# One core, attention and gated unit: head sums on ScalarE, seeded value blocks, joined tails, and a new written order

## The chip, the core and the metric

The kernel runs on one core of a Trainium2 chip. Its time is the device time of one execution in microseconds (us); a kernel's figure is the median of its runs. TensorE multiplies, and writes its results into eight accumulator banks; VectorE and ScalarE read those banks and work element by element; GpSimd and SyncE (SP) mostly issue transfers, and GpSimd also takes powers and copies a few rows. Every engine runs its own list of instructions in order and waits where an operand is not there yet.

## What is computed

Eight batches, eight heads, 576 tokens, head width 64, so 512 channels:

```python
kv  = einsum('bhsd,bhse->bhde', k, v)          # 64x64 per head
out = einsum('bhsd,bhde->bhse', q, kv)
x   = out / sqrt(mean(out*out, -1) + 1e-6) * g_norm    # per head
x   = x.transpose(0, 2, 1, 3).reshape(8, 576, 512)
gate = sigmoid(causal 5-tap convolution of x along the tokens, per channel)
return (gate * (x @ w_val)) @ w_out
```

q, k, v and g_norm are float32. The three weights are double precision and are narrowed to float32 on the chip.

## The kernel before

All work is a list of named steps, PLAN, in an order that is written out: a loop runs it from front to back, each step appends its instructions to the engines' lists, and numbers behind an @ say which of a few fixed buffers (rooms) a new tile takes. So the order of the steps is the order on every engine and every queue. `bank` tiles are the eight accumulator banks.

Per batch b:

- `load_half` brings k or v in two halves of head pairs, `load_q` or `load_q_rows` brings q. `kv_product` makes k'v (L476), `kv_copy` (or `kv_half` for batch 0) moves it out of the bank. `turn_q` (VectorE, L500) or `turn_q_rows` with `sort_q` (TensorE L515 and copies L534, batches 0 and 1) turn q so that the head width lies on the partitions.
- `raw_pair` (two chunks of 128 tokens), `raw_tail` (the last 64 tokens) and, for batch 0, `raw_half` multiply q by kv (L551, L563). A batch has four chunks c = 0 to 3 and the tail c = 4.
- `square` (ScalarE, L600) squares a chunk into a buffer that has one more column per head, holding 64 times 1e-6; `sums` (VectorE, L607) adds up each head's 65 columns; `powers` (GpSimd, L617) raises the sums to −0.5; `normalise` scales: for batch 0 one VectorE instruction per chunk (L626), for the others one ScalarE instruction per chunk and head with the root as a per-partition scale (L636).
- The result is turned so that channels lie on partitions: `turn_x` (TensorE, L648) with `keep_x` (L655) for batches 0 and 1 and for tails, `turn_blocks` (VectorE, L661) with `move_blocks` (transfers, half on SP, half on GpSimd, L669) otherwise. `halo` copies the convolution's earlier rows (GpSimd).
- `gate_start` (ScalarE, L680), four `gate_tap` (VectorE, L686) and `gate_end` (sigmoid on ScalarE, L693) for each of four channel blocks.
- Value product: batches 0 and 1 by `val_product` (L698), each output block the sum of four products with the four row blocks of w_val. From batch 2 on `val_fast` (L747) makes four output blocks from seven products of sums instead of eight: bank a takes products 0, 2, 4 and 6 one on top of the other and is read out between them, b takes product 3, c takes 1 and 5. `x_sums`, `val_sums` make the sums (VectorE); `val_keep` n copies (ScalarE, n = 0, 1, 2, 6) or adds (VectorE, n = 3, 4, 5, L754) into gv.
- `gated` multiplies gate and value (L711). Output: `fast_product i p n` (L838), again seven products, for batches 2i and 2i+1, with `token_sums`, `weight_sums` and `fast_keep`. The 64-token tails of two batches are done together by `out_product i 8` (L785), a plain product with 64 columns of weights per batch, and `keep_out`. `store` writes the rows.
- The weights: `stage_weight` loads one of four column blocks; `narrow_weight ... n` turns it in steps n = 0 to 7, of which 1, 2 and 3 are three ScalarE passes over the exponents (L405, L407, L409) and the others VectorE passes. `start_warm` only multiplies the identity, to occupy TensorE.

The order around the change is given by PLAN alone. Transfers are issued by SP in PLAN's order, except that q's second half and v of batch 0 go by ScalarE's queue, and half of `move_blocks`, the convolution weights and g_norm by GpSimd's.

Of the kernel before, what the change touches and what calls it, by code (L numbers as in the profile page):

```python
# [9 lines left out]
FP32 = mybir.dt.float32  # L10
# [9 lines left out]
load_q_rows 0 1; load_q_rows 0 0; load_half v 0 0 @ 0; load_half k 0 0 @ 0; load_half v 0 1 @ 0;  # L20
load_half k 0 1 @ 0; start_warm 5 256 @ 0; warm_up; stage_weight wval 0; stage_weight wval 1;
stage_weight cw 0 @ 0; turn_q_rows 0 4 @ 1; turn_q_rows 0 3 @ 2; sort_q 0 4 @ 0; turn_q_rows 0 0 @ 3;
turn_q_rows 0 2 @ 4; sort_q 0 3; turn_q_rows 0 1 @ 5; start_warm 3 256 @ 6; load_q_rows 1 0; load_q_rows 1 1;
sort_q 0 0; stage_weight wval 2; kv_product 0 0 @ 7 0; narrow_weight cw 0 0 @ 0; load_half k 1 1; sort_q 0 2;
load_half v 1 1; kv_half 0 0; sort_q 0 1; raw_half 0 3 0 @ 1; narrow_weight cw 0 1; narrow_weight cw 0 2;
kv_product 0 1; stage_weight wval 3; narrow_weight cw 0 3; load_half k 1 0; narrow_weight cw 0 4;
narrow_weight cw 0 5 @ 0; raw_half 0 0 0 @ 2; stage_weight wout 1 @ 1; narrow_weight cw 0 6 @ 1; kv_half 0 1;
narrow_weight cw 0 7; narrow_weight wval 0 0 @ 1; raw_half 0 3 1; narrow_weight wval 0 5 @ 2;
narrow_weight wval 0 1; raw_half 0 0 1; narrow_weight wval 0 6 @ 3; turn_cw @ 6; square 0 3 @ 0;
raw_half 0 2 0 @ 3; keep_cw; square 0 0 @ 1; sums 0 3 @ 0 0; raw_half 0 2 1; narrow_weight wval 0 2;  # L30
raw_half 0 4 1 @ 4; sums 0 0; powers 0 3; load_half v 1 0; square 0 2 @ 2; raw_half 0 4 0;
narrow_weight wval 1 0 @ 0; raw_half 0 1 0 @ 5; square 0 4 @ 0; sums 0 2; narrow_weight wval 0 3;
raw_half 0 1 1; sums 0 4; load_half v 2 1 @ 0; start_warm 1 256 @ 0; narrow_weight wval 1 1;
narrow_weight wval 0 4; powers 0 2; square 0 1 @ 1; narrow_weight wval 1 5 @ 0; narrow_weight wval 1 2;
narrow_weight wval 0 7; stage_weight wout 0 @ 2; turn_q_rows 1 3 @ 7; normalise 0 3 @ 0;
narrow_weight wval 1 3; turn_q_rows 1 2 @ 6; sums 0 1; sort_q 1 3 @ 1; turn_q_rows 1 1 @ 0;
load_half v 2 0 @ 0; narrow_weight wval 2 0 @ 1; turn_x 0 3 @ 1; narrow_weight wval 1 6 @ 1; powers 0 1;
normalise 0 4 @ 1; narrow_weight wval 2 1; turn_q_rows 1 0 @ 7; load_q 2 2; normalise 0 2 @ 2; turn_x 0 4 @ 4;
keep_x 0 3; narrow_weight wval 1 4; turn_x 0 2 @ 3; keep_x 0 4; narrow_weight wval 2 2;
narrow_weight wval 2 5 @ 2; kv_product 1 1 @ 1 4; narrow_weight wval 1 7; keep_x 0 2;  # L40
narrow_weight wval 2 6 @ 3; sort_q 1 1; val_product 0 1 1 @ 3; narrow_weight wval 3 0 @ 0;
narrow_weight wval 3 5 @ 0; halo 0; normalise 0 1 @ 0; narrow_weight wval 3 1; normalise 0 0 @ 1;
narrow_weight wval 2 3; narrow_weight wval 3 6 @ 1; turn_x 0 1 @ 0; narrow_weight wval 3 2; turn_x 0 0 @ 5;
narrow_weight wval 2 4; load_half k 2 1 @ 0; val_product 0 0 1 @ 2; keep_x 0 1; narrow_weight wout 1 5 @ 2;
# [186 lines left out]
def kernel(  # L231
# [22 lines left out]
    HALO = (K - 1) * TB  # L254
    SX = HALO + S
    HB = P // TB
    NV = 2
    NR = S // D
    SV = S // NV
    ACT_NORM = range(1, B)  # L260
    WHOLE = (0,)
    TURNED_X = 2
    FAST_VAL = 2
    FAST_OUT = 0
    PAIRED_Q = (0, 1)
    ACT_SUMS = ()
# [69 lines left out]
    def head(hp, r):  # L336

        return r * (H // 2) + hp
# [579 lines left out]
```

## Time and profile before

| | |
|---|---|
| three runs | 295.33 us median (295.32 to 295.54) |
| profiled execution, first to last instruction | 294.9 us |
| TensorE busy | 287.0 us, 97% |
| VectorE busy | 268.7 us, 91% |
| ScalarE busy | 198.7 us, 67% |
| GpSimd busy | 120.7 us, 41% |
| first value product (L698) starts | 26.97 us |
| last product ends | 290.5 us |
| four tail products (L785) | 14.6 us |
| 32 head sums of eight heads (L607) | 21.6 us |

The profile takes one execution. Busy time counts an engine from the start of an instruction to its end, overlaps once. A group's line gives source line, engine, operation, what is written from what, shapes, count, busy time, mean ns of one, and the engine's idle time before it with what ended it. The chain follows back from the last instruction what released each step. A float32 product is recorded as two matmul records, a transpose as one.

### The profile page before, as it was taken

The page shows a single profiled execution, that of the slowest core. Times are in us where ns is not written, and L with a number is a line of the kernel's source. Part 1 is how long each engine was busy: PE and PEld are TensorE (multiplying, and loading weights), DVE is VectorE, ACT ScalarE, POOL GpSimd, SP SyncE. Part 2 cuts the span into 40 slices and gives each one's busy share as a digit, 9 for nine tenths or more (in the row PEclk, how much of TensorE's full clock was granted, in tenths as well). Part 3 has the DMA queues.
Part 4 walks back from the last instruction along what each step waited for, and adds up shares of the span by engine and source line. Part 5 has one row for each costly group of instructions (what it writes and reads, how often), then busy time and mean ns, then how long its engine had stood idle before and what let it go on. Part 6 is the DMA issues. An engine that isn't in the chain of part 4 may idle for free.

```text
span 294.9 us, 8675 instructions
## 1 busy us (share of the span) xinstructions
PE 287.0 (97%) x3279; PEld 226.9 (77%) x3279; DVE 268.7 (91%) x483; ACT 198.7 (67%) x621; POOL 120.7 (41%) x131
## 2 busy tenths in 40 slices
PE   7999999999999999999999999999999999999994
PEld 3776878788887768878887767888887588788583
DVE  1699999999999999999999999999998999999812
ACT  2899999999786667867477576659588433723330
POOL 3067054854491477421881649021592072000020
PEclk9997999999999999999999999999999999999999
DMA  7999998886686766946789789534553170221344
GB/s 268 379 392 410 284 276 230 239 258 176 197 189 198 234 150 182 341 144 174 182 237 279 167 218 308 165 112 109 141 128 80 44 170 2 57 53 36 98 105 120
DMA packets 32009, 55.51 MB, mean 188 GB/s; under 512 B 6166, under 2 KB 14358, under 8 KB 31968
## 3 DMA queue, kind: packets, MB, share of 16 engines
q1 hardware_dynamic: 29328, 49.50, 57.2%
q0 software_dynamic: 1760, 3.43, 5.2%
q10 hardware_dynamic: 880, 2.03, 1.8%
q8 instruction: 26, 0.43, 0.6%
q14 instruction: 15, 0.12, 0.1%
HBM read 39.21 MB, written 9.44 MB: 165 GB/s over the span
## 4 chain that ended last, share of the span: by engine, by line
PE 94%; DMA 2%; ACT 1%; DVE 1%; issue 0%
PE bank L838 33%; PE bank L747 28%; PE bank L698 11%; PE bank L476 7%; PE bank L551 6%; PE bank L785 5%; PE bank L648 2%; DMA qs<-in_q_dram 2%; PE bank L563 2%; PE bank L515 1%; PE bank L464 0%; ACT wexp L409 0%; DVE x L626 0%; ACT sq L596 0%; DVE ss L607 0%; ACT wexp L407 0%
## 5 line engine op out<-in xcount | busy, mean ns | idle before, releaser
L617 POOL TENSOR_TENSOR rt<-ss,mhalf 128x8 f32<-128x8 f32 (+3 forms) x38 | 73.1, 1937 | 82.0 <-DVE ss L607 81.8
L686 DVE SCALAR_TENSOR_TENSOR gate<-xT,cwT,gate 128x576 f32<-128x576 f32 x128 | 100.4, 807 | 0.2
L636 ACT ACTIVATE x<-bank,rt 128x64 f32<-128x64 f32 x252 | 56.1, 375 | 3.5 <-POOL rt L617 3.2
L838 PE MATMUL bank<-wsum,w 128*128 128x256 f32 x192 | 47.3, 381 | 0.0
L669 POOL DMA_DIRECT2D xT<-y x48 | 26.6, 559 | 41.6 <-DVE gv L754 13.5
L838 PEld LDWEIGHTS bank<-wsum,w 128*128 128x128 f32 x192 | 36.0, 190 | 6.1 <-issue 0.8
L747 PE MATMUL bank<-xs,vsum 128*128 128x288 f32 x144 | 37.1, 407 | 0.0
L747 PEld LDWEIGHTS bank<-xs,vsum 128*128 128x128 f32 x144 | 27.3, 190 | 7.3
L698 PE MATMUL bank<-xT,wval 128*128 128x288 f32 x128 | 32.8, 411 | 0.0
L838 PE MATMUL bank<-wout,gv 128*128 128x256 f32 x128 | 32.3, 382 | 0.0
L698 PEld LDWEIGHTS bank<-xT,wval 128*128 128x128 f32 x128 | 24.0, 192 | 6.3
L693 ACT ACTIVATE gate<-gate 128x576 f32<-128x576 f32 x32 | 23.0, 727 | 7.9 <-DVE gate L686 7.8
L838 PEld LDWEIGHTS bank<-wout,gv 128*128 128x128 f32 x128 | 24.0, 190 | 3.5
L680 ACT ACTIVATE gate<-xT,cwT 128x576 f32<-128x576 f32 x32 | 25.2, 804 | 0.9 <-DVE gv L711 0.9
L747 PE MATMUL bank<-xT,wval 128*128 128x288 f32 x96 | 25.7, 406 | 0.0
L600 ACT ACTIVATE sq<-bank 128x256 f32<-128x256 f32 (+1 forms) x70 | 21.6, 400 | 6.0 <-PE bank L551 5.8
L711 DVE TENSOR_TENSOR gv<-gv,gate 128x576 f32<-128x576 f32 x32 | 23.5, 745 | 2.0 <-ACT gate L693 1.5
L607 DVE TENSOR_REDUCE ss<-sq 128x8 f32<-128x520 f32 (+1 forms) x40 | 24.7, 624 | 0.5 <-ACT sq L600 0.4
L848 DVE TENSOR_TENSOR ot<-bank,ot 128x256 f32<-128x256 f32 (+1 forms) x32 | 17.2, 546 | 8.4 <-PE bank L838 4.1
L747 PEld LDWEIGHTS bank<-xT,wval 128*128 128x128 f32 x96 | 18.2, 190 | 4.5
L854 ACT COPY ot<-bank 128x256 f32<-128x256 f32 x16 | 6.0, 376 | 22.6 <-PE bank L838 22.6
L551 PEld LDWEIGHTS bank<-kv,qT 64*64 64x64 f32 x1008 | 16.3, 135 | 4.8 <-issue 2.1
(91 smaller groups left out, 469.4 us busy)
## 6 DMA issues: line engine op xcount, KB each, us to landing
qs<-in_q_dram SPq DMA_DIRECT2D x96, 140.0 KB, 4.0
out_dram<-ot SPq DMA_DIRECT2D x136, 64.0 KB, 1.7
k<-in_k_dram SPq DMA_DIRECT2D x14, 576.0 KB, 4.9
v<-in_v_dram SPq DMA_DIRECT2D x12, 576.0 KB, 5.3
xT<-y POOLq DMA_DIRECT2D x48, 64.0 KB, 2.7
xT<-y SPq DMA_DIRECT2D x48, 64.0 KB, 2.7
y<-in_moe_w_val_dram SPq DMA_DIRECT2D x4, 512.0 KB, 11.9
w<-in_moe_w_out_dram SPq DMA_DIRECT2D x4, 512.0 KB, 7.1
```

What stands on the lines that cost most here:

```text
L551: nc.tensor.matmul(st["raw", b, c][r][cols, to * D:(to + 1) * D], st["qT", b][rows, hp, first:first + D], kvs[b % 2][rows, hp, :], start=T ...
L607: nc.vector.reduce_sum(out=st["ss", b][:, FIRST[c]:FIRST[c] + n], in_=st["sq", b, c][:, 0:n], axis=AX.X)
L617: nc.gpsimd.tensor_tensor(out=st["rt", b][:, which], in0=st["ss", b][:, which], in1=mhalf[:, which], op=ALU.pow)
L636: nc.scalar.activation(out=x[:, to * D:(to + 1) * D], in_=raw[:, h * D:(h + 1) * D], func=AF.Copy, scale=root[:, to:to + 1])
L669: (nc.sync if i % 2 else nc.gpsimd).dma_start(out=xTs[b % 2][i * TB:(i + 1) * TB, :, first:first + P], in_=y[a * TB:(a + 1) * TB, i])
L680: nc.scalar.activation(out=gate[:], in_=xTs[b % 2][:, jt, HALO:SX], func=AF.Copy, scale=cwT[:, K - 1, jt:jt + 1])
L686: nc.vector.scalar_tensor_tensor(out=gate[:], in0=xTs[b % 2][:, jt, tap * TB:tap * TB + S], scalar=cwT[:, tap, jt:jt + 1], in1=gate[:], op ...
L693: nc.scalar.activation(out=gate[:], in_=gate[:], func=AF.Sigmoid)
L698: nc.tensor.matmul(val[:], wval[:, kc, jt * P:(jt + 1) * P], xTs[b % 2][:, kc, HALO + n * SV:HALO + (n + 1) * SV], start=(kc == 0), stop=( ...
L711: nc.vector.tensor_tensor(out=both, in0=both, in1=st["gate", b, jt][:], op=ALU.mult)
L747: nc.tensor.matmul(st[bank, "val", b, mj][:], weights_[:, k], tokens()[:, k], start=(n in (0, 1, 3) and k == 0), stop=(k == NK // 2 - 1), ...
L838: nc.tensor.matmul(st[bank, i, p], tokens()[:, k], weights_[:, k], start=(n < 2 and k == 0), stop=(k == NK // 2 - 1), skip_group_check=True)
```

## The change

- *Head sums.* For batches 1 to 7 `square` makes one ScalarE instruction per head, whose accumulator output is the head's sum; the squares themselves go to a scrap buffer. `sums` is gone for them, and GpSimd adds 64 times 1e-6 before the power.
- *Batch 0 in whole-array units.* Four units (two chunk pairs by two halves of the heads) of two chunks each: `raw_unit`, `square_unit`, `sums_unit`, `powers_unit`, `normalise_unit`, `turn_unit`, `keep_unit`. A unit needs only half of the heads' kv. `val_product` of batch 0 can run in two halves; the weights' row blocks are paired as 0, 2 and 1, 3 (EARLY, LATE) in place of 0, 1 and 2, 3.
- *Loads.* The second half of k of batch 0 is loaded behind the first column block of w_val; later loads change places as well.
- *Seeded value blocks.* In twelve blocks `val_keep 0` copies bank a into bank b, and product 3 is accumulated on top; then one copy replaces the addition.
- *Joined tails.* `keep_tail` gathers the tails of two batches; two such pairs go through the seven-product form as `fast_product 4 0 n` and `5 0 n`; `out_product` and `keep_out` are no longer in the list.
- *Narrowing.* Steps 2 and 3 become one VectorE pass (minimum, then times 2^23).
- *Choice of engine.* Many copies, `normalise` and `gate_start` take a flag that puts them on VectorE; `move_blocks` is split into its SP and GpSimd halves.
- The whole PLAN is written in a new order.

```diff
-load_q_rows 0 1; load_q_rows 0 0; load_half v 0 0 @ 0; load_half k 0 0 @ 0; load_half v 0 1 @ 0;
-load_half k 0 1 @ 0; start_warm 5 256 @ 0; warm_up; stage_weight wval 0; stage_weight wval 1;
...
+load_q_rows 0 0; load_q_rows 0 1; start_warm 1 248 @ 0; load_half k 0 0 @ 0; load_half v 0 0 @ 0; load_half v 0 1 @ 0;
...
+kv_product 0 0 @ 2 3; kv_half 0 0 0; start_warm 1 254 @ 4; stage_weight wval 0; load_half k 0 1 @ 0; turn_cw @ 1;
+kv_half 0 0 1 1; raw_unit 0 0 @ 5; keep_cw; narrow_weight wval 0 5 @ 2; sort_q 0 1; narrow_weight wval 0 0 @ 1;
...
+powers 5 1; normalise 5 1 @ 2; store 0 7; gate_tap 3 2 3; fast_product 1 0 2; turn_blocks 5 0; fast_keep 1 0 2;
...
+fast_keep 3 3 4; store_last 3 6 0; start_warm 1 244 @ 7; fast_product 3 3 6; store_last 3 6 1; fast_keep 3 3 6 1;
+store_last 3 7 1; store_last 3 7 0
...
-    ACT_SUMS = ()
-    ROOTS = {(0, 2): H + H // 2, (0, 1): 2 * H}
+    ACT_SUMS = (1, 2, 3, 4, 5, 6, 7)
+    SEEDED_OUT = set()
+    SEEDED_VAL = {(4, 0), (7, 1), (2, 1), (3, 1), (6, 1), (7, 0), (2, 0), (5, 1), (3, 0), (5, 0), (6, 0), (4, 1)}
...
+    def copy(e, out, in_):
+
+        if e:
+            nc.vector.tensor_copy(out=out, in_=in_)
+        else:
+            nc.scalar.copy(out=out, in_=in_)
...
         elif n == 2:
-            nc.scalar.activation(out=e, in_=e, func=AF.Relu, bias=biases[0:rows, 1:2], scale=-1.0)
-        elif n == 3:
-            nc.scalar.activation(
-                out=e, in_=e, func=AF.Identity, bias=biases[0:rows, 2:3], scale=-float(1 << 23))
+            nc.vector.tensor_scalar(
+                out=e, in0=e, scalar1=MOST, scalar2=float(1 << 23), op0=ALU.min, op1=ALU.mult)
...
         if b in ACT_SUMS:
             new_sums(b)
+            first = columns(b, c).start
             for r, raw in enumerate(st["raw", b, c]):
                 for h in range(n // 2):
                     to = r * n // 2 + h
                     nc.scalar.activation(
-                        out=sq[:, to, 0:D], in_=raw[:, h * D:(h + 1) * D], func=AF.Square,
-                        accum_out=st["ss", b][:, FIRST[c] + to:FIRST[c] + to + 1])
+                        out=junk[:, h], in_=raw[:, h * D:(h + 1) * D], func=AF.Square,
+                        accum_out=st["ss", b][:, first + to:first + to + 1])
             return
...
+    def root(b, which):
+        ss, rt = st["ss", b][:, which], st["rt", b][:, which]
+        if b in ACT_SUMS:
+            nc.gpsimd.tensor_scalar_add(ss, ss, D * EPS)
+        nc.gpsimd.tensor_tensor(out=rt, in0=ss, in1=mhalf[:, which], op=ALU.pow)
...
+    def raw_unit(g, i):
+
+        raw = st["unit", g, i] = ps([P, 2, C // 2], f"unit{g}_{i}")
+        for j, c in enumerate(UNIT[g]):
+            for m in range(2):
+                nc.tensor.matmul(
+                    raw[:, j, m * P:(m + 1) * P], st["qT", 0][:, 2 * i + m, c * P:(c + 1) * P],
+                    kv_bd[:, 2 * i + m, :], start=True, stop=True)
...
+    def normalise_unit(g, i):
+        x = st["ux", g, i] = new("x", [P, 2, C // 2], FP32, f"ux{g}_{i}")
+        roots = st["rt", 0][:, unit_columns(g, i)]
+        for j in range(2):
+            scaled(x[:, j].rearrange("p (r h e) -> p r h e", r=2, e=D), st["unit", g, i][:, j],
+                   roots[:, j * H // 2:(j + 1) * H // 2])
+
+    def turn_unit(g, i):
+        px = st["upx", g, i] = ps([P, 2, 2, P], f"upx{g}_{i}")
+        for j in range(2):
+            for r in range(2):
+                nc.tensor.transpose(px[:, r, j, :], st["ux", g, i][:, j, r * P:(r + 1) * P], ident[:])
...
-    def val_product(b, jt, n):
-        val = ps([P, SV], f"val{b}_{jt}_{n}")
-        for kc in range(NK):
+    def val_product(b, jt, n, i=None):
+        if ("val", b, jt, n) not in st:
+            st["val", b, jt, n] = ps([P, SV], f"val{b}_{jt}_{n}")
+        for kc in range(NK) if i is None else (i, i + NK // 2):
...
+        begins = (0, 1) if (b, mj) in SEEDED_VAL else (0, 1, 3)
+        if n in begins:
             st[bank, "val", b, mj] = ps([P, SV], f"v{bank}{b}_{mj}")
...
+    def val_keep(b, mj, n, on=0):
+        seeded = (b, mj) in SEEDED_VAL
+        if seeded and n == 0:
+            st["b", "val", b, mj] = ps([P, SV], f"seed{b}_{mj}")
...
         if n == 0:
-            nc.scalar.copy(out=to(0, 0), in_=a)
+            copy(on, out=b_ if seeded else to(0, 0), in_=a)
...
+        elif n == 3 and seeded:
+            copy(on, out=to(0, 0), in_=b_)
...
+    def keep_tail(b, on=0):
+
+        if ("tail", b // 2) not in st:
+            st["tail", b // 2] = new("sq", [P, NK, P], FP32, f"tail{b // 2}")
+        first = b % GVS * S + SF
+        copy(
+            on, out=st["tail", b // 2][:, :, b % 2 * T:(b % 2 + 1) * T], in_=gv[:, :, first:first + T])
...
+        chunk = lambda r, k: lambda: (
+            gv[:, k, begin + r * P:begin + (r + 1) * P] if i < B // 2 else st["tail", 2 * (i - B // 2) + r][:, k])
```

More of the change, by code (lines that the diff above doesn't have):

```diff
@@ L576, with columns @@
     FIRST = {3: 0, 2: H, 4: 2 * H, 1: 2 * H + H // 2, 0: 3 * H + H // 2}
+    def columns(b, c):
+        first = NJ * H if b in WHOLE else FIRST[c]
+        return slice(first, first + heads(c))
     def new_sums(b):
@@ L654, in keep_x @@
         px = st["px", b, c][:].rearrange("p k t -> p (k t)")[:, 0:NK * m]
[L655 to L658 removed]
+        copy(on, out=xTs[b % 2][:, :, first:first + m], in_=px.rearrange("p (k t) -> p k t", k=NK))
     def turn_blocks(b, c):
@@ L859, in fast_keep @@
         else:
-            last = (i, p) == (B // 2 - 1, 2 * NV - 1)
-            (nc.vector.tensor_copy if last else nc.scalar.copy)(out=second[:, LOW], in_=a)
+            copy(on, out=second[:, LOW], in_=a)
     def store_last(i, c, n):
```

644 lines of the change are left out of this document (333 added, 311 removed).

## The prediction

> **What bounds the kernel now.** I read the page first, then the busy time by stretches, the groups of instructions, the chain in order of time, and for prices the timeline of ScalarE.
>
> ```profile
> span 294.9 us, 8675 instructions
> PE 287.0 (97%) x3279; PEld 226.9 (77%) x3279; DVE 268.7 (91%) x483; ACT 198.7 (67%) x621; POOL 120.7 (41%) x131
> PE 94%; DMA 2%; ACT 1%; DVE 1%; issue 0%
> ```
> ```profile
> core 0: us, PE busy (x) PEld busy (x) DVE busy (x) ACT busy (x) POOL busy (x), PEclk, DMA share, GB/s
> 0.00:27.00 27.00, 23.49 (x320) 16.57 (x320) 17.43 (x57) 20.05 (x50) 11.70 (x14) 0.95 0.97 357
> 27.00:80.00 53.00, 53.00 (x897) 42.87 (x894) 52.08 (x92) 50.05 (x159) 23.46 (x20) 0.99 0.85 247
> 80.00:140.00 60.00, 60.00 (x741) 48.24 (x740) 59.93 (x105) 44.33 (x151) 30.76 (x33) 1.00 0.71 201
> 140.00:220.00 80.00, 80.00 (x1005) 64.83 (x1004) 79.42 (x136) 52.85 (x180) 42.08 (x46) 1.00 0.69 187
> ```
> ```profile
> L607 DVE TENSOR_REDUCE ss<-sq 128x8 f32<-128x520 f32 x32 | 21.6, 679 | 0.1
> L636 ACT ACTIVATE x<-bank,rt 128x64 f32<-128x64 f32 x252 | 56.1, 375 | 3.5 <-POOL rt L617 3.2 <-DVE y L661 0.3
> ```
> ```profile
> 17.89 0.39 ACT sq L596
> 18.28 0.61 ACT wexp L409
> 18.89 0.61 ACT wexp L405
> 21.40 0.68 DVE ss L607
> 104.55 3.58 PE bank L785 x16
> 206.62 12.29 PE bank L838 x56
> 290.56 0.42 DVE ot L861
> ```
> ```profile
> DVE wexp L400 <- DMA w<-in_moe_conv_w_dram: 6.8, 1, 6.8
> ```
> ```profile
> 46.92 1.74 ACT L636 ACTIVATE x<-bank,rt 128x64 f32<-128x64 f32 x8
> 49.71 1.12 ACT L655 ACTIVATE xT<-bank 128x512 f32<-128x512 f32 x2
> 146.35 1.21 ACT L600 ACTIVATE sq<-bank 128x256 f32<-128x256 f32 x4 [0.27 <-PE bank L551]
> ```
>
> TensorE is busy for all of 27 to 290.6 us and holds 94% of the chain: its list of work sets the end. VectorE is full beside it until 220 us, ScalarE almost full until 80. Only the head (3.5 us of TensorE idle, plus warm-up products) and the last 4.3 us are anything else; from 17.9 to 24 us the chain runs over ScalarE and VectorE.
>
> A row's mean includes overlap with the next instruction, so I price by distances from start to start: a 64-column activation 0.20 us ((1.74 − 0.375)/7), a head-sum reduce 0.60, a gate tap 0.73. With such prices I counted both written orders. "Behind" is an engine's work listed before a step; "lost" is the step's start minus it.
>
> Before, at raw_tail 1, 2, 3, 4, 7 (starts 37.7, 75.5, 103.0, 133.4, 232.1 us): TensorE has 22.8, 60.0, 87.0, 117.4, 215.7 us behind it, so it has lost 14.9, 15.5, 16.0, 16.0, 16.4; VectorE 26.0, 64.2, 91.6, 121.9, 219.0, lost 11.7, 11.3, 11.4, 11.5, 13.1; ScalarE at the first two 30.3 and 66.8, lost 7.4 and 8.7. At the last product TensorE has done 273.7 and lost 16.8.
>
> **The change, part by part.**
>
> *Joined tails.* Four tail products (4 × 3.58 = 14.3 us of TensorE) become two seven-product blocks, 56 records; the chain row of exactly 56 such records is 12.3 us, and 56 × 0.216 is 12.1. On the path: −2.1. VectorE gets eight half-size sums (2.7) and the blocks' additions (1.9); ScalarE eight tail copies (2.2) and loses four 0.48 copies.
>
> *Head sums.* VectorE loses 28 reduces of 0.60 and seven of 0.33: −19.1. ScalarE loses 70 squares (56 × 0.26 + 14 × 0.17 = 17.1) and gets 252 one-head squares with an accumulator, an operation that the trace does not have. Bounds: two 512-column copies are 0.46 apart and 256-column squares 0.26, which leaves about 0.10 for 64 columns if the accumulator is free; the full 0.375 of L636 if nothing overlaps. I take 0.20, L636's distance: the nearest row, 64 columns with something extra for each head. At that price +50.4. GpSimd gets 35 small adds ahead of its powers, 0.1 to 0.6 each (its 128x124 copies take 0.57); it is 41% busy and the adds only lengthen a latency.
> [...]
>
> *Narrowing weights.* Two ScalarE passes (0.61 + 0.62, nine times: −11.1) become one VectorE pass (+3.1). Both were on the chain between 18 and 21 us.
>
> *Seeded blocks.* Twelve VectorE additions (0.37) become twelve ScalarE copies (0.29): −4.4 and +3.5. New wait: product 3 of a block waits for ScalarE's copy of bank a, and all later TensorE work queues behind it. Between the end of product 0 and product 3 lie 1.1 us of other products at blocks (2,1) and (3,1), 3.4 to 5.6 at the other ten; the copy takes 0.42. At (3,1) a gate start (0.68) and a copy stand ahead of it on ScalarE, about even with the cover. I take 0; without cover, about 0.5 each.
>
> *Choices of engine.* Four normalisations, eight late copies and others go to VectorE (+5.1), ScalarE −6.3 for the normalisations. Totals: TensorE 273.7 → 271.5, VectorE 266.1 → 255.4, ScalarE 185.9 → 155.3 + 252p (205.7 at p = 0.20).
>
> *The head.* Moved on SP's queue: k's second half goes behind the first value weights, q of batch 1 behind one more 512 KB weight block (about 1.3 us later at the page's 392 GB/s), k and v of batch 1 after that; ScalarE's queue is as before; GpSimd's halves of the block moves become steps of their own. VectorE starts on q at about 6.9 us instead of waiting to 8.5 for the convolution weights. Following the new list with the rows' durations, the last transpose that batch 0's value products need comes at about 25 us with 13.2 us of TensorE work behind it (lost 11.8; before, the first value product at 27.0 had lost 14.3). But then kv_product 1 0 waits for loads I put at 28 us, and raw_tail 1 for ScalarE's last sort at about 33.5. Most of the head's gain is spent there.
>
> *What VectorE allows.* New list at raw_tail 2, 3, 4, 7: TensorE 37.4, 71.3, 99.3, 182.3 behind, VectorE 43.8, 73.6, 101.9, 187.8. Of the direct needs the tightest is the product 0 1 1 behind weight_sums 3: VectorE's list is 7.4 ahead of TensorE's there (before: 4.9), elsewhere at most 5.5. I put VectorE's loss at 9.5 (6.9 start, some 2.6 of waits; before 11.4). So TensorE has lost about 7.4 + 9.5 − 0.8 = 16.1 there, the 0.8 being what the same sum overshoots before; before it was 15.9. At the end I take 16.5 against 16.8: −0.3, with bounds −2.5 (VectorE loses only 8, GpSimd never late) and +2.5 (it loses as much as before).
>
> *The end.* One more warm-up product and the wait of the last product for VectorE's addition just ahead of it: +0.5 (0 to 0.8). The last copy and store stay, 4.4 us after the last product.
>
> Sum: −2.1 − 0.3 + 0.5 = −1.9, on the profiled span 294.9: 293.0. The median of the runs is 0.45 above that span, so **293.4**.
>
> **Rivals.**
>
> *ScalarE becomes the bound: slower.* The place is from kv_product 4 1 (behind batch 3's normalisation) on, with 104 head squares done. At p = 0.20 ScalarE's list is 5.0 us ahead of TensorE's there, and before, 7.5 ahead was borne at raw_tail 1 without idle TensorE. Each 0.01 in p is 1.0 us there and 2.5 us further on (all 252). So it decides from p = 0.225; at 0.25 the lead is 10.1 and +2.6 eats the gain; at 0.275 13.5, at 0.30 17.5 (+10: 303.4), at 0.375 over 320. If the accumulator costs an instruction of its own, as short as the 0.16 between 128-column squares, p = 0.26: +4, **297.4**. For it: ScalarE full until 80 us already. Against it: 30.6 us of other ScalarE work goes away.
> [...]
>
> *VectorE stays the bound: no change or slightly slower.* It loses 11.4 in its head again, because GpSimd's five powers in a row (1.7 to 2.0 each) hold up the normalisations. Then the 7.4 at weight_sums 3 costs +2 and the end comes at **295.4**. For it: the list does VectorE work earlier than before; against: 10.7 less of it in all.
>
> *A larger gain.* The weight sums are not late and the head's lead is kept: loss 14.5, **291.4**. For it: the chain's 6 us over narrowing passes; against: loads in the head already run at 357 GB/s with the DMA engines 97% busy.
>
> **How the numbers follow.** A change under 0.2% (0.6 us) is about what a measurement cannot tell from none. TensorE-bound as summed: 0.46, range 292 to 294.6. Larger gain: 0.08. VectorE stays the bound: 0.16, of it 0.10 within 0.2% and 0.06 above. ScalarE bound: 0.24, 296 to 304 and beyond. Other waits of the new order (seeds, banks), 296 to 298: 0.06. Faster 0.54, same 0.10, slower 0.36. The range 291.0 to 302.0 leaves out some 0.05 below and 0.10 above.
>
> **What would show it.** Right: the tail products' 14.3 us gone and 56 more product records at 0.216; TensorE at full in the stretches from 27 us on; ScalarE nearly full to about 110 us, head squares 0.20 apart; VectorE at its first sort near 7 us; the reduces down to five. Wrong: a separate accumulator row on ScalarE, TensorE waiting for normalisations or seed copies between 80 and 200 us, or its first value products in a row no earlier than 27 us.

## The result, and the profile after

The changed kernel takes 299.11 us (median; 298.0 to 299.98) against 295.32 for the kernel before on the same chip: 1.0118 of its time, 95% interval 1.0090 to 1.0146. Run again on another chip: 300.04 against 295.48, 1.0139 [1.0107, 1.0172]. It is slower by about 4 us, where 1.9 us less was forecast.

Three parts of the page of the changed kernel, engines, chain and groups:

```profile
span 297.2 us, 9102 instructions
PE 287.1 (97%) x3283; PEld 233.2 (78%) x3283; DVE 260.6 (88%) x476; ACT 216.8 (73%) x1020; POOL 133.5 (45%) x164
PE 85%; DMA 8%; ACT 3%; issue 1%; SPq 0%; DVE 0%; ACTq 0%
...
L602 ACT ACTIVATE junk<-bank 128x64 f32<-128x64 f32 x252 | 54.0, 326 | 5.0 <-PE bank L558 5.0
L602 ACT ACTIVATION_READ_ACCUMULATOR junk<-bank 128x1 f32 x252 | 53.4, 312 | 0.1
L624 POOL TENSOR_SCALAR ss<-ss 128x8 f32<-128x8 f32 (+1 forms) x35 | 17.0, 485 | 49.5 <-ACT junk L602 48.1
```

TensorE is still the engine that sets the end, but its share of the chain falls from 94% to 85%: loads take 8%, "issue" 1%. Most of those loads, 19.3 of 24.9 us, stand in the head (v of batch 0 to 9.6 us, q of batch 1 to 20.6 us); the rest is v of batch 7, below. VectorE gave up 8 us of busy time, ScalarE took 18 more. Each head square now has a second instruction, the read of its accumulator.

The busy time by stretches of the changed kernel:

```profile
core 0: us, PE busy (x) PEld busy (x) DVE busy (x) ACT busy (x) POOL busy (x), PEclk, DMA share, GB/s
27.00:47.00 20.00, 20.00 (x436) 16.44 (x438) 19.95 (x40) 19.22 (x104) 11.23 (x12) 1.00 0.97 318
47.00:57.00 10.00, 7.40 (x238) 6.26 (x227) 8.30 (x16) 8.67 (x40) 3.77 (x6) 1.00 0.90 245
57.00:80.00 23.00, 23.00 (x292) 18.29 (x291) 21.91 (x40) 21.82 (x131) 17.17 (x20) 1.00 0.70 193
80.00:140.00 60.00, 59.89 (x853) 49.41 (x852) 59.02 (x100) 54.93 (x302) 40.94 (x51) 1.00 0.86 242
140.00:220.00 80.00, 79.35 (x894) 65.06 (x893) 78.56 (x132) 70.69 (x353) 49.49 (x63) 1.00 0.62 167
```

The largest loss stands in ten microseconds: TensorE works 7.40 of the 10 from 47 to 57 us, and no other engine is full there. The chain in order of time (start, duration, what) says what ended it:

```profile
45.81 1.78 PE bank L481 x109
47.59 2.07 issue
49.66 0.79 PE bank L481 x35
...
53.47 1.31 PE bank L558 x77
54.78 0.53 issue
55.30 1.26 PE bank L558 x67
```

"Issue" is time in which the engine waited for nothing that the profile shows. The two pieces, 2.07 and 0.53 us, make up the 2.60 that are missing. They fall inside `kv_product` (L481) and `raw_tail` (L558), in the middle of products that need nothing new. What it waits for is in the list of DMA queues of 47.0 to 48.3 us (packets, MB, share of the 16 engines):

```profile
q1 hardware_dynamic: 95, 0.28, 77.4%
q8 instruction: 1, 0.02, 5.6%
```

One packet of 16 KB of instructions stands among 95 packets of data on q1. Two such packets end at 48.26 and 53.82 us, and TensorE goes on 1.40 and 1.48 us later. Counting TensorE's instructions (weight loads, matmuls, its semaphore events), the two waits come at number 1474 and 1730: 256 apart.

The second place is at 160 to 175 us of the same chain:

```profile
165.88 5.60 DMA v<-in_v_dram
171.48 0.14 issue
171.62 2.33 PE bank L481 x144
```

`kv_product 7 1` starts 0.14 us after v of batch 7 landed; TensorE stood idle for 0.65 us there. The load itself was issued at 165.88 us, behind four stores on SP, and the chain reaches these over head squares and a seed copy on ScalarE. When the same kernel ran again, TensorE went on there without such a wait: this place is tight rather than held by one load.

The forecast counted TensorE's work listed before a step and called the rest of its start "lost". The same count at the same steps (us lost; the last two columns are kernels whose edits follow below, without the loads of q for batches 2 to 7):

| step | before | changed | changed, again | changed without q | before without q |
|---|---|---|---|---|---|
| raw_tail 1 | 14.9 | 13.6 | 13.7 | 13.6 | 13.1 |
| kv_product 2 0 | 15.3 | 13.6 | 13.8 | 13.6 | 13.5 |
| raw_tail 2 | 15.5 | 16.0 | 16.1 | 14.3 | 14.3 |
| raw_tail 3 | 16.1 | 17.7 | 17.0 | 15.2 | 14.9 |
| raw_tail 4 | 16.0 | 17.9 | 18.1 | 15.5 | 14.8 |
| kv_product 7 1 | 16.0 | 19.9 | 20.1 | 17.1 | 14.7 |
| raw_tail 7 | 16.4 | 20.3 | 20.6 | 17.3 | 15.5 |
| end of the last product | 16.8 | 21.4 | 21.7 | 18.8 | 15.9 |

To 46 us the changed kernel stands better by 1.7 us than the profile of before; it then loses 2.4 us up to raw_tail 2, 3.9 more to `kv_product 7 1`, and 1.5 after that.

One correction on the before column. In every run here but those of one kernel (no_tails, 1.8 to 2.7), time minus span is 1.7 to 1.9 us. Of 66 runs of the kernel before, 58 have spans of 293.0 to 294.2, and seven, with a mean granted clock of 0.992 or 0.993, have 294.6 to 294.9: its profile, span 294.9 at 0.993, is of the second kind, about 1 us longer than usual. The cause is seen in it: a window at half the granted clock, which the profile of the kernel before without q (same median time as before) does not have. These are the two kernels, in this order, in the same stretch:

```profile
24.30:27.70 3.40, 3.40 (x78) 2.81 (x77) 3.40 (x8) 3.34 (x9) 3.37 (x5) 0.50 1.04 413
```
```profile
24.30:27.70 3.40, 3.40 (x83) 2.86 (x83) 3.40 (x8) 3.34 (x8) 3.09 (x5) 1.00 1.03 412
```

So the last column shows the usual execution of before better: at raw_tail 1 the changed kernel is not 1.3 us ahead but 0.5 behind.

### The profile page after: what moved, and what is told of

Same layout as the page of the kernel before. It is cut to its first block, busy times and chain, and to the rows that moved or that the text cites. A ratio compares the mean times of both kernels' runs of the same rounds, so it can differ in the third digit from the quotient of the medians.

```text
span 297.2 us, 9102 instructions
## 1 busy us (share of the span) xinstructions
PE 287.1 (97%) x3283; PEld 233.2 (78%) x3283; DVE 260.6 (88%) x476; ACT 216.8 (73%) x1020; POOL 133.5 (45%) x164
## 3 DMA queue, kind: packets, MB, share of 16 engines
q1 hardware_dynamic: 29520, 49.76, 57.1%
## 4 chain that ended last, share of the span: by engine, by line
PE 85%; DMA 8%; ACT 3%; issue 1%; SPq 0%; DVE 0%; ACTq 0%
PE bank L920 34%; PE bank L805 26%; PE bank L756 11%; PE bank L481 6%; PE bank L558 5%; DMA v<-in_v_dram 5%; DMA qs<-in_q_dram 4%; ACT junk L602 3%; PE bank L705 1%; PE bank L469 1%; PE bank L520 1%; ACT x L653 1%; SPq L961 0%; PE bank L694 0%; ACT ot L341 0%
## 5 line engine op out<-in xcount | busy, mean ns | idle before, releaser
L625 POOL TENSOR_TENSOR rt<-ss,mhalf 128x8 f32<-128x8 f32 (+1 forms) x40 | 72.6, 1822 | 15.3 <-DVE ss L678 12.4
L602 ACT ACTIVATE junk<-bank 128x64 f32<-128x64 f32 x252 | 54.0, 326 | 5.0 <-PE bank L558 5.0
L602 ACT ACTIVATION_READ_ACCUMULATOR junk<-bank 128x1 f32 x252 | 53.4, 312 | 0.1
L920 PE MATMUL bank<-wsum,w 128*128 128x256 f32 x216 | 53.2, 381 | 0.0
L653 ACT ACTIVATE x<-bank,rt 128x64 f32<-128x64 f32 x220 | 50.9, 434 | 0.9 <-POOL rt L625 0.6
L341 ACT COPY ot<-bank 128x256 f32<-128x256 f32 x63 | 26.1, 442 | 28.9 <-PE bank L920 28.3
L920 PEld LDWEIGHTS bank<-wsum,w 128*128 128x128 f32 x216 | 40.3, 190 | 6.5 <-issue 0.2
L341 ACT COPY gv<-bank 128x288 f32<-128x288 f32 x63 | 28.2, 452 | 21.7 <-PE bank L805 21.5
L624 POOL TENSOR_SCALAR ss<-ss 128x8 f32<-128x8 f32 (+1 forms) x35 | 17.0, 485 | 49.5 <-ACT junk L602 48.1
L920 PE MATMUL bank<-wout,gv 128*128 128x256 f32 x128 | 32.7, 381 | 0.0
L756 PEld LDWEIGHTS bank<-xT,wval 128*128 128x128 f32 x128 | 23.7, 190 | 6.0
L920 PEld LDWEIGHTS bank<-wout,gv 128*128 128x128 f32 x128 | 24.1, 190 | 3.8
L750 ACT ACTIVATE gate<-gate 128x576 f32<-128x576 f32 x32 | 23.6, 774 | 3.3 <-DVE gate L743 3.3
```

What stands on the lines that cost most here:

```text
L341: nc.scalar.copy(out=out, in_=in_)
L602: nc.scalar.activation(out=junk[:, h], in_=raw[:, h * D:(h + 1) * D], func=AF.Square, accum_out=st["ss", b][:, first + to:first + to + 1])
L625: nc.gpsimd.tensor_tensor(out=rt, in0=ss, in1=mhalf[:, which], op=ALU.pow)
L653: nc.scalar.activation(out=x[:, to * D:(to + 1) * D], in_=raw[:, h * D:(h + 1) * D], func=AF.Copy, scale=roots[:, to:to + 1])
L750: nc.scalar.activation(out=gate[:], in_=gate[:], func=AF.Sigmoid)
L756: nc.tensor.matmul(st["val", b, jt, n][:], wval[:, kc, jt * P:(jt + 1) * P], xTs[b % 2][:, kc, HALO + n * SV:HALO + (n + 1) * SV], start=( ...
```

## The experiments

Ratios are to the kernel before on the same chip, with 95% intervals. Where nothing else is said the edit is made to the changed kernel. A wait is given as the time in which TensorE is idle; the expectations, put down before each run, count from the last product's issue in some places, which gives 0.2 to 0.4 us more. A profile is of one execution, and its time is given where it lies 2 us or more from the median.

### Idle products that shift TensorE's code

If the waits come where a block of code ends, extra instructions ahead of them move the waits to other work. Twenty idle instructions more, then sixty, in place of three warm-up products of about the same duration:

```diff
-start_warm 3 256 @ 3
+start_many 8 96 @ 3      # pe_shift20
+start_many 18 43 @ 3     # pe_shift60
```

> The changed kernel with one difference: three idle warm-up products of 256 columns at 3.85 us become eight of 96 columns, the same columns, 20 more TensorE instructions (weight loads and products). Theory A (TensorE runs dry of instructions): the two stalls of the changed kernel at 47.4 and 54.6 us lie exactly 256 TensorE instructions apart, and TensorE goes on 1.4 to 1.5 us after a 16 KB packet of the instruction queue has ended; so the block ends move 20 instructions earlier in the list, and by the delays of the fetches seen in the changed kernel the stalls become about 0.5 us near 41, 1.1 near 47.8 and 0.8 near 54 us: 297.5 to 299.5. Theory B (the stalls are waits for data or for another engine at these steps): the same stalls at the same products, 299.1 within 0.5.

> As the last one, with eighteen warm-up products of 43 columns: 60 more TensorE instructions. Theory A: with block ends 60 instructions earlier the same delays of the fetches give stalls of about 1.5 us near 15, 4.9 near 38, 1.2 near 58 and up to 2.4 more in the rest, and none at the second half of k and v of batch 2: 301 to 308. Theory B: 299.1 within 0.5, the 2.07 us stall stays between the 37th and the 38th record of kv_product 2 1.

pe_shift20: 303.0 us, 1.0274 [1.0239, 1.0310]; its profile is a run of 300.4. pe_shift60: 312.37 us, 1.0529 [1.0483, 1.0574]. The waits moved into other steps, as a fetch would have it, but not at constant cost: pe_shift20 has one of 1.45 us at 40.87 and one of 2.31 at 172.85, where none was foreseen. The chain of pe_shift20, then of pe_shift60 and two windows behind its wait:

```profile
38.44 2.42 PE bank L762 x10
40.87 1.45 issue
42.32 0.51 PE bank L762
```
```profile
34.98 2.24 PE bank L564 x139
37.22 3.80 issue
41.02 0.48 PE bank L564 x4
```
```profile
41.00:44.40 3.40, 3.38 (x11) 2.48 (x12) 2.19 (x4) 0.00 (x0) 1.51 (x1) 0.50 0.73 221
44.40:48.00 3.60, 3.60 (x11) 2.59 (x10) 0.67 (x2) 2.05 (x17) 0.20 (x1) 0.66 0.16 51
```

In pe_shift60 the waits stand at instruction 450, 1218, 3009, 3777 and 4546, all 449 + 256k to within one. After the longest, the granted clock is half until 46.8 us; TensorE works 5.8 us at it, which by estimate costs 2.5 to 2.9 us more (72 products of `kv_product` took 2.13 us at half the clock in the kernel before, at 24.91 us, and 1.21 at the full one, at 32.33). The place of the block ends alone, with the same work in the same order, is worth 3 to 13 us.

Is the kernel before spared by its code or by luck?

```diff
-start_warm 5 256 @ 0
+start_many 20 64 @ 0     # in the kernel before
```

> The kernel before, its first five idle warm-up products of 256 columns written as twenty of 64, the same columns: 60 more TensorE instructions and nothing else. Theory A (TensorE's code comes in blocks of 256 instructions, and each fetch waits behind the loads): the block ends move into other steps; with the fetch delays of the trace of before the waits become about 2.0 us near 15, 0.3 near 148 and 2.5 near 171 us: about 300.5 (298 to 304), where the kernel before has 295.7. If only the changed kernel's order is at fault: 295.7 within 0.4.

298.04 us, 1.0091 [1.0078, 1.0104]. The old order waits at its block ends too (instructions 450 and 4802), only less long, 0.80 and 0.47 us. The first:

```profile
13.89 1.69 PE bank L569 x10
15.58 0.80 issue
```

Sixty instructions cost the old order 2.6 us, of which its profile shows 1.3 as such waits, and the new one 12 to 13. How long a fetch waits after TensorE has crossed the end of the block before explains part of it: 1.0 to 2.2 us in the kernel before at 32 to 51 us, 3.2 to 4.7 in the changed kernel at 28 to 55.

### Two theories on other engines

```diff
+pad 16   # twice: 16 small ScalarE copies                      (act_pad)
-accum_out=ss[...]   +nc.vector.memset(ss, 1.0)                 (no_accum)
```

> The changed kernel with 32 one-column copies added on ScalarE (two groups of 16, about 3 us each, in stretches near 262 and 282 us where ScalarE is 10% busy). All four runs of the changed kernel lie 1.8 us above their spans, the kernel before 0.45 above its own, and an 8 KB packet of the other instruction queue starts 0.3 us behind the changed kernel's last record. Theory C (that packet is ScalarE's next block of code, needed for its last few instructions): 32 instructions earlier the block comes while ScalarE idles, the time outside the span falls to about 0.5 us and the median to 297.7 (297.2 to 298.3). Rival (the 1.8 us are something else): the time outside the span stays 1.8, 299.1 to 299.6.

307.74 us, 1.0332 [1.0289, 1.0375]; the profile is a run of 310.01. It was to lengthen ScalarE's code and with it the time outside the span. That stayed at 1.8 us, so no part of the loss lies there. The run says nothing more: the copies delayed work of the list, and TensorE waited 2.91 us at 270 us.

> The changed kernel with the head squares written without their accumulators, so the head sums are left out and constants are used in their place: ScalarE has 252 accumulator reads of 0.093 us less, 23 us of its work. Theory A (TensorE's code fetches and late loads hold it): 299.1 within 0.7, the stalls of 2.07 and 0.74 us stay. Rival (ScalarE is the bound that the accumulators made, as in the prediction's first rival): the time falls by 2 us or more, to 297 or less, because TensorE no longer waits behind normalisations from 84 us on.

299.1 us, 1.0095 [1.0068, 1.0122]: the time of the changed kernel, though ScalarE is busy 18 us less.

```profile
PE 286.3 (96%) x3283; PEld 232.7 (78%) x3283; DVE 260.6 (88%) x478; ACT 198.6 (67%) x768; POOL 133.6 (45%) x164
```

The wait for code stays (1.95 us at 47.90), and the one ahead of `kv_product 7 1` is 1.65 us here. That ScalarE's accumulator sets the time is not borne out; that it costs a little, hidden behind a longer wait elsewhere, one profile cannot exclude.

### The loads: leaving some out

```diff
 def load_q(b, ...):
+    if b == 2: continue      # no_q2
+    if b >= 2: continue      # no_q; before_no_q in the kernel before
```

> The changed kernel without the sixteen loads of q of batch 2 (560 KB, issued from 29 to 45 us), so that batch computes on other numbers. Theory A2 (the fetch is late because it stands behind loads): the fetch that belongs to the second half of k and v of batch 2 starts earlier than the 4.4 to 4.8 us after the last block end that all six profiles of this order show, by 2 us or more, the wait there falls from 2.07 to under 0.5 us, and the time to 296.5 to 298. Rival (the fetch is late whatever is loaded): the delay stays 4 us or more, the time 298.5 to 299.5.

300.29 us (295.87 to 301.82), 1.0105 [1.0073, 1.0137]. Its profile, a run of 295.87, has no wait at `kv_product 2`; its nine runs spread over 6 us. One execution supports the theory and the median doesn't, so the three runs that follow were made together.

> The changed kernel itself, beside the others on their chip. Theory: its time hangs on when the late loads and code blocks come, so it spreads more than the kernel before: a median of 298.5 to 302, runs 2 us or more apart, where those of the kernel before lie within 1 us. If the edited kernels (undone tails, undone seeds) were truly 5 us slower, the median stays near 299.1 with runs within 1 us.

300.04 us, as told above: the control on that chip.

> The changed kernel without the 96 small loads of q of batches 2 to 7 (3.4 MB of 49 MB on SP's queue, and 96 of its issues), so those batches compute on other numbers. If the loads are the common cause: no wait over 0.5 us at kv_product 2 and at kv_product 7, TensorE has lost about 14.5 us at 66 us and under 18 at its last product, and the time is 293.5 to 296, at or below the kernel before. If the order itself is at fault (VectorE, ScalarE, banks): 298 or more.

296.91 us, 1.0055 [1.0038, 1.0073]: 3.1 us less than the control, and a spread of 1.5 us where the control has 4.9. These loads are larger than the expectation says: queue q1 moves 35.99 MB without them and 49.76 with them, so 13.8 MB and not 3.4.

> The kernel before without the same 96 loads. Its TensorE list is full from 27 us on and its code waits are under 0.3 us, so under either theory nothing is gained: 294.5 to 295.7.

295.48 us, 0.9994 [0.9979, 1.0009]: nothing. The same loads cost the new order 3.1 us and the old one nothing. The stretches of the changed kernel without q:

```profile
27.00:80.00 53.00, 52.92 (x959) 42.40 (x958) 52.49 (x97) 51.93 (x285) 34.62 (x38) 1.00 0.49 163
80.00:140.00 60.00, 59.73 (x852) 49.46 (x852) 59.33 (x102) 54.98 (x296) 40.41 (x52) 1.00 0.62 174
140.00:220.00 80.00, 79.55 (x898) 65.67 (x897) 78.84 (x131) 69.55 (x345) 44.96 (x61) 1.00 0.42 107
```

The 2.60 us that TensorE lost from 47 to 57 us are gone, with 49% of DMA share from 27 to 80 us where the changed kernel has 84%. The table gives it by place: at raw_tail 2 the changed kernel has lost 1.7 us less without these loads, at kv_product 7 1 2.8, at the end 2.6.

What the loads do is two things: code comes late among them, and SP issues them in order. In the trace of the changed kernel SP's 325 issues take turns on eight semaphores, and at 33.06, 34.96, 36.46, 38.79 and 41.36 us SP issues 0.01 to 0.02 us after the landing of the load that was issued eight before (33.04, 34.94, 36.45, 38.77, 41.34). Whatever stood next in that queue waited for a landing there.

The profiles say which of the two weighs more. The waits for code come to 2.60 us in the changed kernel (2.07 and 0.53) and to 2.56 when it ran again (1.95 and, at 89.72 us, 0.61); without q there is none. The wait for v of batch 7 is 0.65 us in the first, absent in the second, and 0.45 us are idle at that place without q as well, behind a store. So of the 2.6 to 2.9 us that TensorE loses less without q in these profiles, nearly all is code. The medians have not been split in this way.

### The order of loads and products

Each of these moves steps; some warm-up products are joined or left out beside it, so that the number of TensorE's instructions shifts too.

```diff
-kv_product 2 0; kv_product 2 1;              # spread: apart by one value product
+kv_product 2 0; ... val_product 0 2 1 0; kv_product 2 1;
-raw_pair 2 1; ... val_product 1 3 0;
+val_product 1 3 0; raw_pair 2 1;
-start_warm 1 250 @ 1; start_warm 1 252 @ 2; start_warm 3 256 @ 3;
+start_warm 3 424 @ 3;
```

> The changed kernel with warm-up products joined (two groups of five products become three of 424 columns: 16 TensorE instructions less), the second half of kv_product 2 behind the value product that followed it, and raw_pair 2 1 behind val_product 1 3 0. Theory A: the dense 64-column products no longer stand together and the block ends lie 16 instructions later in the list; by the same delays the waits for code sum to 1.8 us where the same sum gives 4.1 for the changed kernel: 296.5 to 297.5. If the code is not what binds, nothing changes: 299.1 within 0.5.

300.18 us, 1.0161 [1.0126, 1.0196]; the profile is a run of 302.33. The wait inside `kv_product 2 1` is 0.60 us in place of 2.07, as it should be when the products use up code less fast, but the whole does not gain. Its chain shows a wait of 0.86 us that was not there:

```profile
163.97 2.08 POOL rt L625
166.28 1.54 ACT x L653 x7
167.82 0.30 ACT gv L341
```

A copy that TensorE waits for (L341) stands on ScalarE behind a normalisation (L653), which waits for GpSimd's addition and power. A longer wait follows ahead of `kv_product 7 1`, 2.09 us at 171.46, with 3.4 us at half the granted clock behind it.

```diff
 load_half k 7 0; +load_half v 7 0; load_half v 7 1    # spread_v7: spread, v ahead of block moves
-start_warm 1 244 @ 7                                 # out in spread_v7 and late6
```

> As the last one, and the two loads of v of batch 7 issued right behind those of k of batch 7, and the last warm-up product left out. The changed kernel waits 0.9 us for v of batch 7 at 170.8 us (2.3 and 1.9 in two other profiles) and its last product waits 0.6 us behind that warm-up product for VectorE. Both gone: 1.0 to 1.5 below the kernel with the spread products alone, 295.2 to 296.4. Rival (VectorE's list is the next bound): the gain is under 0.5.

303.8 us, 1.0293 [1.0268, 1.0319]. v came in time, and the block moves (xT<-y) behind it came late:

```profile
155.04 9.27 DMA xT<-y
...
164.46 2.83 POOL xT L730 x4
...
167.69 1.05 POOL rt L625
```

The adds and powers of GpSimd queue behind its halo copies, and TensorE waits 4.25 us.

```diff
 move_blocks 5 1 1; +load_half v 7 1; load_half v 7 0; load_q 7 0     # late6
-powers 6 1; normalise 6 1 @ 1; ... fast_keep 4 0 0 @ 1;
+powers 6 1; ... fast_keep 4 0 0 @ 1; normalise 6 1 @ 1;
```

> The changed kernel with three moves behind 145 us: the two loads of v of batch 7 issued right behind the block moves of batch 5 and ahead of q of batch 7; normalise 6 1 on ScalarE behind the two copies that TensorE needs (val_keep 4 0 2 and fast_keep 4 0 0); the last warm-up product left out. Theory D (in-order queues in this stretch: SP's loads for batch 7, ScalarE's normalisation waiting for GpSimd in front of a copy): the 0.9 us wait for v at 170.8 us goes, the 0.6 us at the end goes, and the runs lie closer together: 297.0 to 298.2. Rival: VectorE or GpSimd is late there in any case, under 0.5 us gained.

303.75 us, 1.0269 [1.0238, 1.0301]; the profile is a run of 306.27.

```profile
164.64 5.05 DMA v<-in_v_dram
169.71 3.10 DMA out_dram<-ot
172.91 0.37 ACT ot L341
173.28 1.65 ACT x L653 x8
```

The normalisation now stands behind a copy into `ot`, whose buffer is free only after a store, which waits on SP behind the loads of v. TensorE waits 3.74 us.

> As the last one, with the spread products and 16 TensorE instructions less of the kernel spread. Spread alone cut the wait at the second half of k and v of batch 2 from 2.07 to about 0.6 us and took away the one of 0.7 at 54.6, and lost it again behind 166 us (1.3 for a ScalarE copy behind a normalisation, 2.0 for v of batch 7, then 3.4 us at half the granted clock). Theories A and D together: 295.2 to 297.0. If the gain of the spread products is always given back: 298 or more.

302.16 us, 1.0183 [1.0161, 1.0205], with both edits: the code wait is 0.60 us, and the wait behind the store 2.63.

> The changed kernel with the kv and raw products of batch 2 spread between four value products (second half of kv_product 2, raw_pair 2 3 and raw_pair 2 1 each behind one), 16 TensorE instructions less in the warm-ups, v of batch 7 loaded right behind the block moves of batch 5, and the last warm-up product left out; normalise 6 1 stays where it was (behind a ScalarE copy that waits for a store it made its own wait of 2 to 4 us). Both places mended by order alone: 295.5 to 297.5. If SP's queue only passes the delay on: 299 or more.

301.93 us, 1.0237 [1.0196, 1.0278], the spread with v behind `move_blocks 5 1 1` and the normalisation left where it was; in its profile, a run of 304.59, TensorE waits 1.66 us at 170.71 for the copy behind that normalisation. None of the five beats the changed kernel: in each profile some other wait of TensorE is longer than in it.

### Parts undone and parts alone

```diff
-token_sums 4 0 n; fast_product 4 0 n; fast_keep 4 0 n     (no_tails; the same for 5 0)
+out_product 0 8; out_product 1 8; keep_out ...; out_product 2 8; out_product 3 8
-SEEDED_VAL = {(4, 0), (7, 1), ...}                        (no_seeds)
+SEEDED_VAL = set()
```

> The changed kernel with the two joined tail blocks undone: four tail products of 16 matmuls from the gathered tails in the places of the blocks' first products, four copies, and no token sums for them. TensorE's work is 2.1 us more by the records, VectorE's 4.6 less. If the tail term of the prediction was right and on the path: 2.1 above the changed kernel on the same chip, 300.5 to 302. Rival (the tails' additions on VectorE cost what TensorE gains): within 0.7 of the changed kernel.

305.91 us, 1.0336 [1.0309, 1.0363]: about 6 above the changed kernel, three times what the records of the tails come to. In its profile, a run of 308.25, TensorE's wait inside `kv_product` at 47.97 us is 2.50, and others stand from 168 to 200 us. The price of the tails cannot be read from this run; it is read below from their records.

> The changed kernel without the seeded value blocks: twelve VectorE additions again in place of twelve ScalarE copies, product 3 into an empty bank. My theory has no wait for seed copies on the path, and VectorE's list has room: 299.1 within 0.7. Rival (the last one of the prediction: product 3 waits for ScalarE's copy): 1 us or more faster.

305.72 us, 1.0346 [1.0322, 1.0370]. Nothing speaks for the rival that the seeds cost time: without them TensorE waits 1.91 and 1.79 us at 102 and 174 us. What they gain can't be read either.

Next the same from the other side, the joined tails in the kernel before, in two forms:

```diff
-out_product 2 8; keep_out 2 8; out_product 3 8; keep_out 3 8     # before_tail23
+keep_tail 4..7; token_sums 5 0 n; fast_product 5 0 n; fast_keep 5 0 n     # at the end
-ACT_SUMS = ()
+ACT_SUMS = (7,)
```

> The kernel before with two of its four tail products (3.58 us each) joined into one block of seven products (28 records, 6.1 us) near the end, and the head sums of batch 7 by ScalarE's accumulator (VectorE 2.7 us less, against 2.3 for the tail's sums and additions). All loads and all TensorE steps ahead of 228 us stay. If the tail term of the prediction holds and the new order is what lost it: 1.1 us faster than the kernel before, 294.0 to 294.8. If a joined block costs as much in waits as it saves: 295.2 or more.

303.3 us, 1.0241 [1.0216, 1.0266]. It runs like the kernel before to 206 us. Then TensorE waits 1.95 us for copies that stand on ScalarE behind head squares. The chain and three stretches:

```profile
205.80 2.64 ACT sq L593 x25
...
209.44 0.26 ACT ot L878
209.71 0.28 ACT ot L867
...
210.03 2.15 PE bank L855 x6
```
```profile
206.00:210.90 4.90, 2.95 (x14) 2.29 (x13) 4.06 (x7) 4.26 (x37) 2.34 (x5) 1.00 0.45 107
210.90:214.30 3.40, 3.40 (x10) 2.66 (x9) 0.00 (x0) 2.56 (x19) 3.31 (x5) 0.50 0.65 151
226.00:250.00 24.00, 21.50 (x106) 16.66 (x105) 23.70 (x38) 12.02 (x40) 8.82 (x14) 1.00 0.30 66
```

Three costs of one edit: the wait, 3.4 us at half the clock behind it, and from 226 us on VectorE full with TensorE at 21.50 of 24. The product that was taken out there had been 3.6 us of TensorE work that gave VectorE time.

> As the last one, and the two last ScalarE narrowing passes of the convolution weights and of the value weights (five blocks, 1.2 us of ScalarE each) made one VectorE pass (0.34 each, 0.2 for the convolution weights). The chain of the kernel before runs over two such passes between 18 and 20 us, so the head may start up to 0.6 us earlier: 293.4 to 294.6. If VectorE, full from 27 us on, pays for it: as the last one, up to 1 us slower.

304.72 us, 1.0291 [1.0264, 1.0318], with the two narrowing passes made one on VectorE as well. The profile shows a window at half clock in the head (23.6 to 27.0 us); no gain of the merged pass is to be seen.

## Why the prediction was wrong, by its own steps

*The baseline* stood on two executions: 0.45 was the distance from the span of one to the time of others. The real distance is 1.8, and the profile was of an execution some 1 us above the median. It carried into "lost 14.9, 15.5, 16.0 …": the usual losses were about 1 to 1.8 lower. Against the usual 15.9 at the end, the forecast "16.5 against 16.8" promised a loss of 0.6, not a gain of 0.3.

*Two sums.* "The 0.8 being what the same sum overshoots before": from the figures given, 4.9 + 11.4 against 15.9, it overshoots by 0.4, so the 16.1 should have been 16.5. And one of the nine narrowing pairs on ScalarE is only 20x128, its passes 0.44 apart, so the −11.1 is 0.4 too large. Neither is near the size of the miss.

*Joined tails, −2.1:* right. The four L785 products (14.34 us) are gone and 56 more records of L920 at 0.220 make 12.3: −2.0.

*Head sums, 0.20 each:* right in size. A square holds ScalarE for 0.103 us to the next start and an accumulator read for 0.093, 0.196 for the pair. The separate accumulator row was listed as a sign that the prediction is wrong, and is there (ACTIVATION_READ_ACCUMULATOR, x252); it does no harm, since square and read together take what was put.

*"ScalarE becomes the bound", 0.24:* the right side, the wrong mechanism: no_accum takes 18 us from ScalarE and the time stays. That 299.1 lies where this rival put it (296 to 304) is luck.

*GpSimd's adds "only lengthen a latency":* they take 0.485 each, and in spread and spread_v7 that latency is on the chain, where a normalisation waits behind add and power with a copy for TensorE queued after it. In the profile of the changed kernel the chain does not pass over them at the two large waits; when it ran again it did, from 161.5 to 168.4 us, with TensorE at work almost throughout.

*Seeds at 0:* no wait of TensorE for a seed copy was found; the changed kernel without them takes 305.72. How much of that is theirs is not settled.

*The head:* in part as put. `kv_product 1 0`, for which loads were "put at 28 us", starts at 28.21; raw_tail 1 at 34.42, for which a sort was put at "about 33.5". But the last transposes (L694), forecast "at about 25 us", start at 26.52, and the first long row of value products (20 records) at 29.37, which was named as a sign of being wrong. At raw_tail 1 nothing of the head's gain is left against the usual 13.1.

*"What VectorE allows": the step that failed.* "16.1" lost at the product behind weight_sums 3, 16.5 at the end, "bounds −2.5 and +2.5". The changed kernel lost 17.4 at that product (16.6 when run again) and 21.4 at the end, outside the upper bound. The term followed VectorE and the direct needs of TensorE; nothing in it could wait for code, and the loads were followed only as far as batch 1's. That "later loads change places as well" was in the change and has no price in the prediction, nor a cover that is named. The line that came nearest, "other waits of the new order (seeds, banks)", had 0.06 and named neither code nor loads. With the loads of q taken away the term holds at that product: 14.8 against 14.4 in the kernel before without q, +0.4 where 16.1 against 15.9 was forecast. At the end it does not hold even then: 18.8 against 15.9.

*The end, +0.5 (0 to 0.8):* right in size. The loss from `fast_product 3 0 0` to the end is 0.92 against 0.34: +0.6.

So the loss at the end grew by 5.5 to 5.8 us (21.4 and 21.7 against the usual 15.9), less 2.1 of listed work: that is, to within 0.1, the +3.3 of the span (297.2 against 293.9, the spans of these two profiles). Of the growth, 2.6 to 2.9 go with the loads of q (the changed kernel against itself without q). The other 2.9 are between the last two columns of the table: 0.3 up to raw_tail 3, 1.5 from there to raw_tail 7, and 1.1 behind it, about half of it the end. Of the 1.5, 0.45 is the idle time ahead of `kv_product 7 1` (to 168.81 us without q), behind a store; the rest no run here assigns.

Still open: what makes a fetch in the old order wait 1 us where DMA share is 1.05 as well (28 to 36 us) and 4 in the new one; why no_q2, whose profile has no wait for code, has a median as high as the changed kernel's; and why the changed kernel without q still gives back the work it saves.

## What to carry to other kernels

Where an engine is full for the whole span, count its instructions as well as its work: here TensorE's code came in 16 KB packets among those of the data (26 on q8 in the changed kernel), and dense small products (72 records in 1.2 us) stood still for 2.07 us under heavy loads (DMA share 0.90 from 47 to 57 us) with every operand ready. So a new order has to be followed through the load queue to its end. Before adding a median and a span, take both from one execution, and look at the granted clock of that execution stretch by stretch. In an order this tight a step taken off the critical engine can remove cover that another engine had, so price what the removed work was hiding.

## What the runs showed of the hardware that was not expected

- TensorE's code came in 16 KB packets (26 on q8 in the changed kernel, 0.43 MB), its waits at instruction 449 + 256k to within one (1474 and 1730 in the changed kernel, five in pe_shift60); in the changed kernel it went on 1.40 and 1.48 us after the packet's end. From the crossing of one block's end to the fetch of a later one 1.0 to 2.2 us passed in the kernel before (32 to 51 us) and 3.2 to 4.7 in the changed one (28 to 55 us).
- The records of the granted clock start at 7.20 (full), 24.27 (half), 27.68 (full) and 293.92 us (half) in the trace of the kernel before, at 7.15 (full) and 297.28 (half) in that of the changed kernel: the distances, 17.07, 3.41, 266.24 and 290.13 us, are whole multiples of 3.41. With steps of that length counted from the first record of each trace, three waits that lie inside one step have half the clock in the next: 2.50 us in late6 (47.90 to 50.40, step 47.82 to 51.23), 2.09 in spread, 1.95 in before_tail23. The same 2.50 us in no_tails (47.97 to 50.48), cut in two by a step's end at 49.48, has the full clock behind it, and so have the changed kernel's 2.07, cut at 48.11. The stretches behind the two waits of 2.50 us, late6 and then no_tails:

```profile
51.20:54.60 3.40, 3.40 (x10) 2.58 (x11) 1.54 (x5) 2.69 (x11) 0.12 (x1) 0.50 1.00 298
```
```profile
50.50:53.90 3.40, 3.40 (x49) 2.81 (x50) 1.66 (x4) 2.59 (x12) 0.89 (x3) 1.00 0.97 280
```

- Each of the 252 activations with an accumulator output on ScalarE in the changed kernel (128x64) has a second record, ACTIVATION_READ_ACCUMULATOR: back to back the activation takes 0.103 us to the next start and the read 0.093.
